# Attention periods of one long kernel: output sums taken from a rotation of three exponent banks, turned 256 columns at a time, and the row of maxima sent one period later

## The chip, the cores and the metric

One NeuronCore of a Trainium2 chip runs one program, of 34,356 recorded instructions. The metric is device time in microseconds, the median of repeated executions. Before the change it is 1423.86 us (three runs, 1423.84 to 1426.14).

## What is computed

Four layers follow each other, A, B, A, B, each added to its input. A is sliding-window attention over 2048 tokens with 576 features, 32 heads of 18, a window of 256; B multiplies the two-dimensional real Fourier transform by a given filter and transforms back. The weights of both A layers are the same, as are the filters of both B layers.

```python
def _A_ref(x, wqkv, wo):
    B, S, D = x.shape
    H = 32; Dh = D // H; W = 256
    qkv = (lambda x, *d: x.transpose(*d))((x @ wqkv).reshape(B, S, 3, H, Dh), 2, 0, 3, 1, 4)
    q, k, v = qkv[0], qkv[1], qkv[2]
    scores = jnp.einsum("bhqd,bhkd->bhqk", q, k) * (Dh ** -0.5)
    idx = jnp.arange(S)
    mask = (idx[:, None] - idx[None, :] >= 0) & (idx[:, None] - idx[None, :] < W)
    scores = jnp.where(mask[None, None], scores, -1e9)
    p = _softmax(scores, axis=-1)
    o = jnp.einsum("bhqk,bhkd->bhqd", p, v)
    return (lambda x, *d: x.transpose(*d))(o, 0, 2, 1, 3).reshape(B, S, D) @ wo
...
x = x + _A_ref(_layernorm(x, axis=-1), A_wqkv, A_wo)
x = x + _B_ref(_layernorm(x, axis=-1), B_w_r, B_w_i)
x = x + _A_ref(_layernorm(x, axis=-1), A_wqkv, A_wo)
x = x + _B_ref(_layernorm(x, axis=-1), B_w_r, B_w_i)
```

The change touches only the attention of the two A layers.

## The kernel before

**Tiles.** An A layer treats its 32 heads as 8 groups n of 4, and the 2048 tokens as 16 tiles of 128; x = 16 n + i counts both, 128 in all. For each x there are four heads (two `pair` by two `hp`), and for each head two products. `score_max` (L1176 on) multiplies queries by keys into a PSUM bank S, up to 128x384, and VectorE (DVE) takes each row's masked maximum out of it: a scan, which also writes its 128x384 by-product to a scratch tile `jk` that nobody reads, and a reading of the engine's accumulator into `m`. The maxima of four tiles are transposed on TensorE (PE) by `m_rows` (L1196), negated on ScalarE (ACT), and sent by DMA into row 63 of the queries, so that the second product already has the maximum subtracted. `exps` (L1206) makes that second product, keys by queries, in a PSUM bank E; ACT exponentiates it into SBUF (P), and GpSimd (POOL) cuts it to the window. `part` (L1228) multiplies P by the values, extended by a column of ones, and accumulates in one bank U: 19 rows for each head, 128 columns for each tile, so U holds four tiles. When these are complete (one x in four) DVE transposes all 512 columns to `us`. `divide` takes the reciprocal of the sums of exponents (DVE) and multiplies (POOL), `back` transposes again (DVE), `store` sends the result.

**Periods.** `mixed()` interleaves this by hand; the order in which the code issues instructions is the order on each engine. A period p handles two x. In it stand 8 scores for x + 10 (LEAD = 10, so maxima are ten tiles ahead of the exponents), 8 exponents, and up to 14 half steps of the query and key projection of later groups (`pj` and `pk`, matmuls with 64 of the 128 rows each). At its end come the 32 matmuls into U (`pv`, for the two x before). There are 59 periods (MIX = 118) in each layer A; p = 0 has no U matmuls, p = 2 to 48 carry projection steps and end with U matmuls, and p = 49 to 58 have no steps left. A period's end is called even or odd by p. At even ends before the change, U is complete and transposed, and `m_rows` runs; `divide` follows in the middle of the next period, `back` at that period's (odd) end, `store` in the middle of the one after. Lists named early, mid and end hold such later work by period. Ahead of `mixed`, `opening` makes the first ten tiles' maxima among projection steps; its fourth score of each tile uses U's bank. Behind `mixed`, a short loop does the last ten tiles.

**PSUM.** Eight banks are shared: S three, pj one, E two, U one, pk one. A matmul into a bank waits until that bank has been read by the instruction that empties it: for S the scan of three scores ago, for E the exponent of two ago. U stays one bank through the whole stage, zeroed once per layer by ACT (`sums`), since only 19 of each 32 rows are written and the transpose reads all.

Of the kernel before, what the change touches and what calls it, by code (L numbers as in the profile page):

```python
# [18 lines left out]
NT = 16  # L19
# [846 lines left out]
def layer_a(tc, ident, eps, bp, big, src, dst, wqk_d, wv_d, wo_d, dc_d, gc_d, dram, copy, wvs, second, spectral, share):  # L866
# [17 lines left out]
    if True:  # L884
# [191 lines left out]
        with ExitStack() as c2:  # L1076
# [19 lines left out]
            def proj(i, c, bank=0):  # L1096
# [5 lines left out]
                def mm(s, k, half=None):  # L1102
# [5 lines left out]
                    if s == 0 and half is None:  # L1108
                        box["ps"] = pp.tile([128, 512], F32, tag="E" if bank else "pj", name=f"pj{i}_{c}", bufs=2 if bank else 1)
                    elif s == 0:  # L1110
                        box[half] = pp.tile([128, 512], F32, tag=("pj", "pk")[half], name=f"{('pj', 'pk')[half]}{i}_{c}", bufs=1)
# [63 lines left out]
            def score_max(x, pair, hp):  # L1175

                n, i = divmod(x, NT)
                c, t = divmod(i, 4)
                q, k = qs[n % 2], ks_[n % 2]
                if (n, c) not in ms:  # L1180
                    ms[n, c] = wp.tile([128, 2, 2, 4], F32, tag="m", name=f"m{n}_{c}", bufs=3)
                lo, hi = max(0, i - 2) * 128, (i + 1) * 128
                N = hi - lo
                b = 64 * hp
                four = x < LEAD and pair == hp == 1
                ps = pp.tile([128, 512], F32, tag="U" if four else "S", name=f"S{x}_{pair}_{hp}", bufs=1 if four else 3)
                T.matmul(ps[:, 0:N], q[b:b + 63, pair, i * 128:i * 128 + 128], k[b:b + 63, pair, lo:hi], start=True, stop=True)  # L1187
                jk = wp.tile([128, 384], BF, tag="jk", name=f"jk{x}_{pair}_{hp}", bufs=2)
                V.tensor_tensor_reduce(out=jk[:, 0:N], in0=ps[:, 0:N], in1=mask[:, 384 - N:384], scale=1.0, scalar=-3e38,  # L1189
                                       op0=ALU.add, op1=ALU.max, accum_out=ms[n, c][:, pair, hp, t:t + 1])  # L1190

            def turned(name):

                return pp.tile([128, 4, 128], F32, tag="E", name=name, bufs=2)
# [12 lines left out]
            def exps(x, pair, hp):  # L1207
# [9 lines left out]
                ps = pp.tile([128, 512], F32, name=f"E{x}_{hl_}", **(dict(tag="S", bufs=3) if pair and NX - LEAD <= x else dict(tag="E", bufs=2)))  # L1217
# [9 lines left out]

            def part(x, half):  # L1228
                n, i = divmod(x, NT)

                e = i - i % 2
                j = (i - 1, i - 2 + 2 * (i % 2))[half]
                q0 = e if j < i else i
                q1 = e + 2 if i - 1 == j else q0 + 1
                for h in range(4):
                    if j >= 0:
                        T.matmul(U[32 * h:32 * h + 19, (q0 % 4) * 128:(q0 % 4) * 128 + 128 * (q1 - q0)], vts[n][:, j, h],  # L1237
                                 pt[n, j][:, h, (q0 - j) * 128:(q1 - j) * 128],
                                 start=j == max(e - 1, 0), stop=j == i or (i == e and j == i - 2), skip_group_check=True)
                if half and i % 4 == 3:  # L1240
                    us[n, i // 4] = u = wp.tile([128, NT, 32], F32, tag="us", name=f"us{n}_{i}", bufs=1)
                    V.transpose(u, U.rearrange("r (p n) -> r n p", n=NT))  # L1242

            def pv(x):
                part(x, 0)
                part(x, 1)
# [3 lines left out]
            def divide(n, c):  # L1250
                u = us[n, c]
                rc = wp.tile([128, NT, 1], F32, tag="rc", name=f"rc{n}_{c}", bufs=2)
                V.reciprocal(rc, u[:, :, 18:19])
                (V if n == NQ - 1 else P).tensor_mul(u[:, :, 0:18], u[:, :, 0:18], rc.to_broadcast([128, NT, 18]))

            def back(n, c):
                os[n, c] = o = wp.tile([128, NT, 32], F32, tag="o", name=f"o{n}_{c}", bufs=2)
                V.transpose(o, us[n, c])
# [68 lines left out]
            us, U = {}, None  # L1327

            def sums():
                nonlocal U  # L1330
                U = pp.tile([128, 512], F32, tag="U", name="U", bufs=1)
                A.activation(U, eps.to_broadcast([128, 512]), AF.Copy, scale=0.0)

            def mixed():
# [11 lines left out]
                for p in range(last):  # L1346
# [9 lines left out]
                    run(early, p)  # L1356
                    for i, (f, *a) in enumerate(some):
# [8 lines left out]
                        if i == 0 and p == 0:  # L1366
                            remainders()
                        if i % 2 == 0 and step:
                            pj[at + n](0)
# [12 lines left out]
                    if p == 0:  # L1382
                        sums()
# [3 lines left out]
                    if p % 2 == 0:  # L1387
                        m_rows(*divmod((2 * p + LEAD + 1) // 4, 4))
                        if p:
                            n, c = divmod((2 * p - 1) // 4, 4)  # L1390
                            plan(mid, p + 1, divide, n, c)
# [6 lines left out]
                    behind(2 * p + 1)  # L1398
                assert at == len(pj)
# [43 lines left out]
            for t in range(MIX, NX + 2):  # L1443
                loads(t)
                for pair in range(2):
# [5 lines left out]
                    if pair == 0 and t - 2 < NX:  # L1451
                        pv(t - 2)
# [8 lines left out]
            def bank(tag, name):  # L1461
                return pp.tile([128, 512], F32, tag=tag, name=name, bufs=dict(pj=1, E=2, S=3)[tag])
# [62 lines left out]
```

## Time and profile before

The profiled execution took 1426.9 us by its own clock, of which 1425.2 us are the span that the trace covers. Its mean granted TensorE clock is 0.963 of full speed.

| | of the span |
|---|---|
| layer A's first mixed stage, p = 2 to 48 | 138.8 to 410.8 us |
| its ten periods without projection steps | 410.8 to 478.5 us |
| the second layer's mixed stage | 867.9 to 1140.6 us, then to 1208.9 us |
| chain that ended last, by engine | PE 73%, ACT 14%, DMA 6%, DVE 3% |
| chain, by line | U L1237 13%, E L1219 11%, P (the exponent) L1220 10%, S L1187 5% |
| the scan, L1189 | 1,024 of them, 497.4 us busy, mean 524 ns |
| the exponent, L1220 | 1,024 of them, 442.2 us busy, mean 471 ns |

In the rows of the trace each instruction stands with its start in us from the beginning of the span, its time, engine, line, operation, and result and operands by name (out<-in); the bracket at a row's end gives the wait before it and what ended it. In the waits, "PE E L1219 <- ACT P L1220: 23.3, 91, 0.5" reads: PE's instructions for E at line 1219 were idle 23.3 us in all, 91 times, because ACT's P at line 1220 was not done, at most 0.5 us at a time. PEld are the weight loads, which run beside matmuls. DVE_READ_ACCUMULATOR2 is the reading behind a scan.

### The profile page before, as it was taken

How to read it: one execution, taken by the hardware profiler on the slowest of the kernel's cores; microseconds unless marked ns; L12 is line 12 of the kernel's file. 1: busy time of each engine (PE TensorE's matmuls, PEld its weight loads, DVE VectorE, ACT ScalarE, POOL GpSimd, SP SyncE). 2: the span in 40 equal slices, each digit the busy share in tenths (PEclk: the TensorE clock that was granted, in tenths of full speed). 3: DMA queues.
4: the chain of work that ended last, by engine and by line, in shares of the span. 5: the costliest groups of instructions: out<-in, count | busy, mean ns of one | idle time of the engine just before them, and what ended most of it. 6: DMA issues, size and time to landing. Idle time of an engine off the chain costs nothing.

```text
span 1425.2 us, 34356 instructions
## 1 busy us (share of the span) xinstructions
PE 1342.7 (94%) x11555; PEld 984.8 (69%) x11555; DVE 956.4 (67%) x3132; ACT 813.2 (57%) x1946; POOL 772.5 (54%) x1248
## 2 busy tenths in 40 slices
PE   9999999999999999999999999999999998999998
PEld 8985555555554589975899865555555544698587
DVE  5428777877776577766663167787788766566855
ACT  5624777777765635443355217777777755575223
POOL 2266677777654534467221385677767655312721
PEclk9999999999987799999999999999999976999999
DMA  6757565755555537678863475656554646488875
GB/s 198 213 179 213 168 199 173 219 178 158 173 169 165 170 95 245 196 251 257 273 229 76 141 205 166 189 178 181 173 174 159 183 142 201 135 272 307 296 226 173
DMA packets 179493, 274.31 MB, mean 192 GB/s; under 512 B 67743, under 2 KB 77727, under 8 KB 177989
## 3 DMA queue, kind: packets, MB, share of 16 engines
q1 hardware_dynamic: 167007, 243.63, 54.6%
q0 software_dynamic: 4656, 13.44, 3.6%
q10 hardware_dynamic: 7654, 15.03, 3.0%
q8 instruction: 93, 1.52, 0.5%
q14 instruction: 83, 0.68, 0.2%
HBM read 164.54 MB, written 114.81 MB: 196 GB/s over the span
## 4 chain that ended last, share of the span: by engine, by line
PE 73%; ACT 14%; DMA 6%; DVE 3%; issue 2%; SPq 1%; POOL 0%; ACTq 0%; DVEq 0%
PE U L1237 13%; PE E L1219 11%; ACT P L1220 10%; PE vps L1005 8%; PE pj L1115 8%; PE ops L802 6%; PE S L1187 5%; PE pk L1115 4%; PE po L274 4%; PE pq L524 3%; PE p L503 2%; PE pf L274 2%; PE pi L600 2%; ACT sg L1136 2%; PE pz L312 1%
## 5 line engine op out<-in xcount | busy, mean ns | idle before, releaser
L1189 DVE CUSTOM_DVE_ANT_0 jk<-S,mask 128x384 bf16<-128x384 f32 (+2 forms) x1024 | 497.4, 524 | 105.7 <-PE S L1187 56.3
L1220 ACT ACTIVATE P<-E 128x384 f32<-128x384 f32 (+2 forms) x1024 | 442.2, 471 | 135.7 <-PE E L1219 69.1
L1219 PE MATMUL E<-qs,ks 64*128 64x384 f32 (+2 forms) x1024 | 385.4, 403 | 54.2 <-ACT P L1220 50.5
L1187 PE MATMUL S<-ks,qs 63*128 63x384 f32 (+2 forms) x1024 | 321.1, 373 | 0.8 <-DVE m L1189 0.6
L1219 PEld LDWEIGHTS E<-qs,ks 64*128 64x128 f32 x1024 | 188.9, 191 | 181.1 <-ACT P L1220 156.2
L1222 POOL TENSOR_SCALAR_AFFINE_SELECT P<-P 128x512 f32<-128x512 f32 x256 | 162.4, 634 | 242.8 <-ACT P L1220 230.8
L1237 PE MATMUL U<-P,vq 128*19 128x128 f32 (+1 forms) x3840 | 208.2, 360 | 0.4 <-POOL P L1222 0.2
L1187 PEld LDWEIGHTS S<-ks,qs 63*128 63x128 f32 x1024 | 175.9, 191 | 41.9 <-DVE m L1189 17.8
L1237 PEld LDWEIGHTS U<-P,vq 128*19 128x19 f32 x3840 | 105.5, 106 | 101.6 <-issue 51.1
L1115 PE MATMUL pj<-xh,wqh 64*128 64x512 f32 (+1 forms) x360 | 152.9, 425 | 0.0
L1225 POOL TENSOR_SCALAR_AFFINE_SELECT P<-P 128x512 f32<-128x512 f32 x224 | 143.7, 642 | 0.0
L1115 PE MATMUL pj<-xh,wql 64*128 64x512 f32 (+1 forms) x360 | 142.2, 433 | 0.0
L1115 PE MATMUL pj<-xl,wqh 64*128 64x512 f32 (+1 forms) x288 | 125.6, 436 | 0.0
L802 PE MATMUL ops<-oroom 128*128 128x290 f32 (+1 forms) x812 | 113.9, 297 | 2.9 <-DVE ofree L825 1.7
L802 PEld LDWEIGHTS ops<-oroom 128*128 128x128 f32 x812 | 110.4, 189 | 3.5 <-ACT ofree L836 2.5
L1242 DVE STREAM_TRANSPOSE us<-U 128x512 f32<-128x512 f32 x64 | 45.9, 717 | 73.2 <-PE U L1237 73.1
L1115 PE MATMUL pk<-xh,wqh 64*128 64x512 f32 x230 | 92.0, 400 | 0.0
L1115 PE MATMUL pk<-xh,wql 64*128 64x512 f32 x230 | 90.2, 396 | 0.0
L1189 DVE DVE_READ_ACCUMULATOR2_ANT m<- 128x1 f32 x1024 | 84.9, 83 | 0.0
L1115 PE MATMUL pk<-xl,wqh 64*128 64x512 f32 x184 | 73.2, 398 | 0.0
L1115 PEld LDWEIGHTS pj<-xh,wqh 64*128 64x128 f32 (+1 forms) x360 | 67.0, 186 | 7.1 <-issue 1.3
L1115 PEld LDWEIGHTS pj<-xh,wql 64*128 64x128 f32 (+1 forms) x360 | 66.9, 186 | 5.5
(519 smaller groups left out, 2599.2 us busy)
## 6 DMA issues: line engine op xcount, KB each, us to landing
qk_d<-sg SPq DMA_DIRECT2D x56, 512.0 KB
qs<-qk_d SPq DMA_DIRECT2D x384, 72.0 KB
ks<-qk_d SPq DMA_DIRECT2D x348, 72.0 KB
op_d<-o SPq DMA_DIRECT2D x56, 256.0 KB
v_d<-vt SPq DMA_DIRECT2D x32, 304.0 KB
vq<-v_d SPq DMA_DIRECT2D x16, 608.0 KB
wt<-in_w SPq DMA_DIRECT2D x16, 580.0 KB
ofree<-x SPq DMA_DIRECT2D x16, 580.0 KB
```

The source lines that it names most:

```text
L274: T.matmul(ps[:, c, 0:NF], tail[r] if si == 4 else hl_(si), dcs[b // 2][r, b % 2], start=mi == si == 0, stop=si == 4)
L802: self.nc.tensor.matmul(self.ps[u][n][:, 0:self.n], x, self.w[p][:, (2 * wk + n) * self.n:(2 * wk + n + 1) * self.n], start=first and i == ...
L1005: T.matmul(ps[:, n, 0:288], xT(xk, c), w[:, wk, n * 288:(n + 1) * 288], start=i == 0, stop=i == len(ks) - 1)
L1115: T.matmul(ps.rearrange("r (n p) -> r n p", n=NT) if second else ps, w[r, wk], x[r], start=s == 0, stop=s == len(ks) - 1)
L1187: T.matmul(ps[:, 0:N], q[b:b + 63, pair, i * 128:i * 128 + 128], k[b:b + 63, pair, lo:hi], start=True, stop=True)
L1189: V.tensor_tensor_reduce(out=jk[:, 0:N], in0=ps[:, 0:N], in1=mask[:, 384 - N:384], scale=1.0, scalar=-3e38, op0=ALU.add, op1=ALU.max, accu ...
L1219: T.matmul(ps[:, 0:nq], k[b:b + 64, pair, j * 128:j * 128 + 128], q[b:b + 64, pair, j * 128:j * 128 + nq], start=True, stop=True)
L1220: A.activation(p[:, hl_, 0:nq], ps[:, 0:nq], AF.Exp, scale=SC)
L1222: P.affine_select(out=p[:, :, 0:128], in_=p[:, :, 0:128], pattern=[[0, 4], [1, 128]], compare_op=ALU.is_ge, fill=0.0, base=0, channel_mult ...
L1225: P.affine_select(out=p[:, :, 256:384], in_=p[:, :, 256:384], pattern=[[0, 4], [-1, 128]], compare_op=ALU.is_gt, fill=0.0, base=0, channel ...
L1237: T.matmul(U[32 * h:32 * h + 19, (q0 % 4) * 128:(q0 % 4) * 128 + 128 * (q1 - q0)], vts[n][:, j, h], pt[n, j][:, h, (q0 - j) * 128:(q1 - j) ...
L1242: V.transpose(u, U.rearrange("r (p n) -> r n p", n=NT))
```

## The change

- **Banks.** pj, pk one each and S three stay. U has no bank of its own any more; E has three instead of two. Each period takes a fresh U out of the rotation of E (out of pk's bank behind `mixed`). The fourth score in `opening` uses pk's bank.
- **U by period.** U holds two tiles, 256 columns, and is transposed at the end of every period but p = 0: 128 columns of `us` rows at a time. Its matmuls load 32 weight columns instead of 19 (the following 13 of the next head beside the 19 wanted), so all 128 rows are written and nothing is zeroed. `us` gets two buffers, and its layout has each half in runs of 16, which `back` undoes with a pattern of four dimensions.
- **Division.** The reciprocal is written in place, and `divide` moves from the middle of the next period to a place behind its first score, as does the list "early" with `pack`.
- **Maxima.** `m_rows` moves from the even end to the odd end after it, and takes its bank out of S (out of E while fewer than 70 projection steps are done).
- **Scratch.** `jk` has one buffer instead of two.

```diff
@@ -1106,7 +1106,7 @@
                     if opens and s == 7 and c == 2 and 0 < i < 8:
                         w_split(i + 1)
                     if s == 0 and half is None:
-                        box["ps"] = pp.tile([128, 512], F32, tag="E" if bank else "pj", name=f"pj{i}_{c}", bufs=2 if bank else 1)
+                        box["ps"] = pp.tile([128, 512], F32, tag="E" if bank else "pj", name=f"pj{i}_{c}", bufs=3 if bank else 1)
                     elif s == 0:
                         box[half] = pp.tile([128, 512], F32, tag=("pj", "pk")[half], name=f"{('pj', 'pk')[half]}{i}_{c}", bufs=1)
                     w = wt[i][0] if p == "h" else wt[i][1]
@@ -1183,15 +1183,15 @@
                 N = hi - lo
                 b = 64 * hp
                 four = x < LEAD and pair == hp == 1
-                ps = pp.tile([128, 512], F32, tag="U" if four else "S", name=f"S{x}_{pair}_{hp}", bufs=1 if four else 3)
+                ps = pp.tile([128, 512], F32, tag="pk" if four else "S", name=f"S{x}_{pair}_{hp}", bufs=1 if four else 3)
                 T.matmul(ps[:, 0:N], q[b:b + 63, pair, i * 128:i * 128 + 128], k[b:b + 63, pair, lo:hi], start=True, stop=True)
-                jk = wp.tile([128, 384], BF, tag="jk", name=f"jk{x}_{pair}_{hp}", bufs=2)
+                jk = wp.tile([128, 384], BF, tag="jk", name=f"jk{x}_{pair}_{hp}", bufs=1)
                 V.tensor_tensor_reduce(out=jk[:, 0:N], in0=ps[:, 0:N], in1=mask[:, 384 - N:384], scale=1.0, scalar=-3e38,
                                        op0=ALU.add, op1=ALU.max, accum_out=ms[n, c][:, pair, hp, t:t + 1])
 
             def turned(name):
 
-                return pp.tile([128, 4, 128], F32, tag="E", name=name, bufs=2)
+                return pp.tile([128, 4, 128], F32, tag="E" if done < 70 else "S", name=name, bufs=3)
 
             def m_rows(n, c):
                 q = qs[n % 2]
@@ -1214,7 +1214,7 @@
                     pt[n, j] = wp.tile([128, 4, 384], F32, tag="P", name=f"P{n}_{j}", bufs=6)
                 p = pt[n, j]
 
-                ps = pp.tile([128, 512], F32, name=f"E{x}_{hl_}", **(dict(tag="S", bufs=3) if pair and NX - LEAD <= x else dict(tag="E", bufs=2)))
+                ps = pp.tile([128, 512], F32, name=f"E{x}_{hl_}", **(dict(tag="S", bufs=3) if pair and NX - LEAD <= x else dict(tag="E", bufs=3)))
                 b = 64 * hp
                 T.matmul(ps[:, 0:nq], k[b:b + 64, pair, j * 128:j * 128 + 128], q[b:b + 64, pair, j * 128:j * 128 + nq], start=True, stop=True)
                 A.activation(p[:, hl_, 0:nq], ps[:, 0:nq], AF.Exp, scale=SC)
@@ -1225,6 +1225,8 @@
                         P.affine_select(out=p[:, :, 256:384], in_=p[:, :, 256:384], pattern=[[0, 4], [-1, 128]], compare_op=ALU.is_gt,
                                         fill=0.0, base=0, channel_multiplier=1)
 
+            us, U = {}, None
+
             def part(x, half):
                 n, i = divmod(x, NT)
 
@@ -1234,12 +1236,18 @@
                 q1 = e + 2 if i - 1 == j else q0 + 1
                 for h in range(4):
                     if j >= 0:
-                        T.matmul(U[32 * h:32 * h + 19, (q0 % 4) * 128:(q0 % 4) * 128 + 128 * (q1 - q0)], vts[n][:, j, h],
-                                 pt[n, j][:, h, (q0 - j) * 128:(q1 - j) * 128],
+                        v = vts[n].rearrange("p b h e -> p (b h e)")[:, 19 * (4 * j + h):min(19 * (4 * j + h) + 32, 76 * NT)]
+                        T.matmul(U[32 * h:32 * h + v.shape[1], (q0 - e) * 128:(q1 - e) * 128], v, pt[n, j][:, h, (q0 - j) * 128:(q1 - j) * 128],
                                  start=j == max(e - 1, 0), stop=j == i or (i == e and j == i - 2), skip_group_check=True)
-                if half and i % 4 == 3:
-                    us[n, i // 4] = u = wp.tile([128, NT, 32], F32, tag="us", name=f"us{n}_{i}", bufs=1)
-                    V.transpose(u, U.rearrange("r (p n) -> r n p", n=NT))
+                if half and i % 2:
+                    c, k = i // 4, i // 2 % 2
+                    if k == 0:
+                        us[n, c] = wp.tile([128, NT, 32], F32, tag="us", name=f"us{n}_{c}", bufs=2)
+                    V.transpose(us[n, c][:, 8 * k:8 * k + 8].rearrange("r b (a p) -> r (b a) p", a=2), U[:, 0:256].rearrange("r (p n) -> r n p", n=NT))
+
+            def sums(tag, x):
+                nonlocal U
+                U = pp.tile([128, 512], F32, tag=tag, name=f"U{x}", bufs=3 if tag == "E" else 1)
 
             def pv(x):
                 part(x, 0)
@@ -1249,13 +1257,13 @@
 
             def divide(n, c):
                 u = us[n, c]
-                rc = wp.tile([128, NT, 1], F32, tag="rc", name=f"rc{n}_{c}", bufs=2)
-                V.reciprocal(rc, u[:, :, 18:19])
+                rc = u[:, :, 18:19]
+                V.reciprocal(rc, rc)
                 (V if n == NQ - 1 else P).tensor_mul(u[:, :, 0:18], u[:, :, 0:18], rc.to_broadcast([128, NT, 18]))
 
             def back(n, c):
                 os[n, c] = o = wp.tile([128, NT, 32], F32, tag="o", name=f"o{n}_{c}", bufs=2)
-                V.transpose(o, us[n, c])
+                V.transpose(o.rearrange("r n (k p) -> r k n p", k=2), us[n, c].rearrange("r (k b) (a p) -> r k (b a) p", k=2, a=2))
 
             def store(n, c, engines=None):
                 o = os[n, c].rearrange("r n p -> r (n p)")
@@ -1324,13 +1332,6 @@
                 for lag, f in zip((1, 3, 4), (divide, back, store)):
                     steps.setdefault(k + lag, []).append((f, n, c))
 
-            us, U = {}, None
-
-            def sums():
-                nonlocal U
-                U = pp.tile([128, 512], F32, tag="U", name="U", bufs=1)
-                A.activation(U, eps.to_broadcast([128, 512]), AF.Copy, scale=0.0)
-
             def mixed():
                 nonlocal done
                 last = MIX // 2
@@ -1353,7 +1354,6 @@
                         some += [(score_max, y, 0, 1), (exps, x, 0, 0), (score_max, y, 1, 1), (exps, x, 1, 0),
                                  (exps, x, 0, 1), (score_max, y, 0, 0), (exps, x, 1, 1), (score_max, y, 1, 0)]
                     n = 0
-                    run(early, p)
                     for i, (f, *a) in enumerate(some):
                         if i in (0, 8):
                             loads(2 * p + i // 8)
@@ -1363,8 +1363,9 @@
                             pj[at + n](1)
                             n += 1
                         f(*a)
-                        if i == 0 and p == 0:
+                        if i == 0:
                             remainders()
+                            run(early, p)
                         if i % 2 == 0 and step:
                             pj[at + n](0)
                         if i == 7:
@@ -1379,16 +1380,17 @@
                             plan(mid, p + 1, f)
                         plan(mid, p + 2, send)
                     ended.clear()
-                    if p == 0:
-                        sums()
+                    if p:
+                        sums("E", p)
                     for x in (2 * p - 2, 2 * p - 1):
                         if x > 0 and x % NT:
                             pv(x)
-                    if p % 2 == 0:
-                        m_rows(*divmod((2 * p + LEAD + 1) // 4, 4))
+                    if p % 2:
+                        m_rows(*divmod((2 * p + LEAD - 1) // 4, 4))
+                    else:
                         if p:
                             n, c = divmod((2 * p - 1) // 4, 4)
-                            plan(mid, p + 1, divide, n, c)
+                            plan(early, p + 1, divide, n, c)
                             plan(end, p + 1, back, n, c)
                             plan(mid, p + 2, store, n, c)
                             if c == 3:
@@ -1396,6 +1398,7 @@
                                     plan(early, p + 4 + h, pack, n, h)
                     run(end, p)
                     behind(2 * p + 1)
+                m_rows(*divmod((2 * last + LEAD - 1) // 4, 4))
                 assert at == len(pj)
                 for d, lags in ((mid, (1, 4)), (end, (3,)), (early, (2, 3))):
                     for k, p in enumerate(sorted(d)):
@@ -1449,6 +1452,8 @@
                     for f, *a in steps.pop(now, ()):
                         f(*a)
                     if pair == 0 and t - 2 < NX:
+                        if t % 2 == 0:
+                            sums("pk", t)
                         pv(t - 2)
                         if t % 4 == 1 and t - 2 < NX - 4:
                             later(now, *divmod(t // 4 - 1, 4))
@@ -1459,7 +1464,7 @@
                 behind(t)
             assert not due and not steps
             def bank(tag, name):
-                return pp.tile([128, 512], F32, tag=tag, name=name, bufs=dict(pj=1, E=2, S=3)[tag])
+                return pp.tile([128, 512], F32, tag=tag, name=name, bufs=1 if tag == "pj" else 3)
 
             out.early(0, [bank(k, f"ops0_{k}") for k in ("pj", "S")], slice(0, 4))
             divide(NQ - 1, 3)
```

In the diff `sums` is defined further up than before (its old definition, from the hunk at L1324, goes), and two hunks at its end take U out of pk behind `mixed` and give the next layer's banks their new counts.

The orders below show the same places of the first layer before and after. A row has the line, the operation, the result's and operands' names (with running numbers) and the shape; x4 means four like it. First PE at the end of the even period p = 4, from the last score to the middle of the next period. Before:

```order
L1187 MATMUL S_1_0_2077<-ks_1061,qs_1059 128x384
L1237 MATMUL U<-P_5_1822,vq_1436 19x256 x4
L1237 MATMUL U<-P_4_1776,vq_1436 19x128 x4
L1237 MATMUL U<-P_6_1887,vq_1436 19x256 x4
L1237 MATMUL U<-P_7_1939,vq_1436 19x128 x4
L1199 MATMUL tpm_0_2099<-ident,m_0_1882 16x128
L1187 MATMUL S_0_1_2109<-ks_1061,qs_1059 128x384
L1219 MATMUL E_0_2114<-qs_1058,ks_1060 128x384
L1187 MATMUL S_1_1_2117<-ks_1061,qs_1059 128x384
```

And after:

```order
L1187 MATMUL S_1_0_2080<-ks_1061,qs_1059 128x384
L1240 MATMUL U_2084<-P_5_1823,vq_1436 32x256 x4
L1240 MATMUL U_2084<-P_4_1777,vq_1436 32x128 x4
L1240 MATMUL U_2084<-P_6_1884,vq_1436 32x256 x4
L1240 MATMUL U_2084<-P_7_1933,vq_1436 32x128 x4
L1187 MATMUL S_0_1_2106<-ks_1061,qs_1059 128x384
L1219 MATMUL E_0_2113<-qs_1058,ks_1060 128x384
L1187 MATMUL S_1_1_2116<-ks_1061,qs_1059 128x384
```

The transpose of the maxima (tpm) is gone from this end; it stands behind the U matmuls of the odd end now, one period later.

Second, DVE at the same even end, from the last scan on; a row of L1189 with jk is a scan, the one with m alone the reading. Before:

```order
L1189 ISA jk_1_0_2079,m_0_1882<-S_1_0_2077,mask 128x384
L1189 ISA m_0_1882 128x1
L1242 STREAM_TRANSPOSE us_7_2097<-U 128x512
L1189 ISA jk_0_1_2111,m_1_2108<-S_0_1_2109,mask 128x384
L1189 ISA m_1_2108 128x1
L1189 ISA jk_1_1_2119,m_1_2108<-S_1_1_2117,mask 128x384
L1189 ISA m_1_2108 128x1
```

And after:

```order
L1189 ISA jk_1_0_2082,m_0_1877<-S_1_0_2080,mask 128x384
L1189 ISA m_0_1877 128x1
L1246 STREAM_TRANSPOSE us_1_1987<-U_2084 128x256
L1189 ISA jk_0_1_2108,m_1_2105<-S_0_1_2106,mask 128x384
L1189 ISA m_1_2105 128x1
L1261 RECIPROCAL us_1_1987<-us_1_1987 128x16
L1189 ISA jk_1_1_2118,m_1_2105<-S_1_1_2116,mask 128x384
L1189 ISA m_1_2105 128x1
```

The transpose is half as wide, and the reciprocal has come forward to a place behind the first scan (it stood behind the fourth).

Third, DVE at the odd end after that, p = 5. Before:

```order
L1189 ISA jk_1_0_2193,m_1_2108<-S_1_0_2191,mask 128x384
L1189 ISA m_1_2108 128x1
L1258 STREAM_TRANSPOSE o_1_2212<-us_7_2097 128x512
L1189 ISA jk_0_1_2222,m_1_2108<-S_0_1_2220,mask 128x384
L1189 ISA m_1_2108 128x1
```

And after:

```order
L1189 ISA jk_1_0_2189,m_1_2105<-S_1_0_2187,mask 128x384
L1189 ISA m_1_2105 128x1
L1246 STREAM_TRANSPOSE us_2_2209<-U_2192 128x256
L1266 STREAM_TRANSPOSE o_1_2217<-us_1_1987 128x2x16x16
L1189 ISA jk_0_1_2227,m_1_2105<-S_0_1_2225,mask 128x384
L1189 ISA m_1_2105 128x1
```

A half transpose of U stands ahead of `back` (L1266), and both ahead of the next scan.

Two waits change with the banks. On PE, exponent 2 of a period (the name E_2) waited for ACT's reading of the bank two exponents back; now U is among the three, and E_2 waits for DVE, that is for the transpose. And on DVE each scan carries a wait for DVE's own count: in before the count that it names lies one or two completions ahead of the instruction just before it, and after the change it is the reading just before it in 841 of 1,024 scans, and an earlier one in the others.

## The prediction, made before the changed kernel was run

> **What bounds the kernel now.** I read the busy times first, then the waits, then the mixed stage by stretches, and last single rows of it.
>
> ```profile
> span 1425.2 us, 34356 instructions
> PE 1342.7 (94%) x11555; PEld 984.8 (69%) x11555; DVE 956.4 (67%) x3132; ACT 813.2 (57%) x1946; POOL 772.5 (54%) x1248
> ```
>
> PE looks like the bound, but the edits lie in the two mixed stages (one for each layer A), so these are read by themselves. The rows give start and end, length, then busy time and instructions of PE, PEld, DVE, ACT and POOL, the granted clock, DMA share and GB/s.
>
> ```profile
> 138.80:410.80 272.00, 252.18 (x2801) 157.83 (x2799) 215.32 (x822) 202.70 (x471) 198.05 (x276) 1.00 0.58 182
> 410.80:478.50 67.70, 61.32 (x459) 32.12 (x460) 46.88 (x177) 38.87 (x93) 35.31 (x52) 0.71 0.55 169
> 867.90:1140.60 272.70, 252.88 (x2805) 157.91 (x2807) 215.54 (x823) 203.30 (x471) 193.81 (x268) 1.00 0.57 173
> 1140.60:1208.90 68.30, 61.70 (x455) 31.77 (x454) 47.16 (x177) 39.07 (x93) 35.31 (x52) 0.71 0.54 166
> ```
>
> The first and third stretch are the 47 periods (p = 2 to 48, from one group of U matmuls to the next) that still carry projection steps: 272.0 / 47 = 5.79 us each, with PE idle for 20 us in all. The second and fourth are the ten periods without them, 6.8 us each at a clock of 0.71. DVE is busy 79% of the first stretch, 4.6 us of each period. PE's idle time, in the first layer from 140 to 465 us:
>
> ```profile
> PE E L1219 <- ACT P L1220: 23.3, 91, 0.5
> ```
>
> So PE waits for one thing, an exponent bank that ACT has yet to read: with two banks the matmul of exponent 7 of a period waits until exponent 5 is read. **But DVE has little to spare**, and how closely it packs its maxima is the point on which I rest the forecast:
>
> ```profile
> 253.14 0.08 DVE L1189 DVE_READ_ACCUMULATOR2_ANT m<- 128x1 f32 x1
> 253.14 0.55 DVE L1189 CUSTOM_DVE_ANT_0 jk<-S,mask 128x384 bf16<-128x384 f32 x1
> 253.62 0.08 DVE L1189 DVE_READ_ACCUMULATOR2_ANT m<- 128x1 f32 x1
> 253.62 0.25 DVE L1253 RECIPROCAL rc<-us 128x16 f32<-128x16 f32 x1
> 253.78 0.49 DVE L1189 CUSTOM_DVE_ANT_0 jk<-S,mask 128x384 bf16<-128x384 f32 x1
> ```
>
> A maximum is two instructions, the scan (0.55) and the reading of its accumulator (0.08). The next instruction starts together with the reading, so scans follow each other every 0.48 us; the reciprocal adds 0.16.
>
> **The change, part by part. jk with one buffer.** A scan may now write jk only when the one before has finished. The built program shows it: each scan has a wait on DVE's own semaphore, in an instruction of its own in front; before, that wait names a point one or two completions ahead of the predecessor and is always past; in the change 841 of 1,024 scans wait for the reading right before them, 13 of 16 in two full periods. No scan of before does this. The nearest rows are the same pair of instructions at another place, followed by one that waits for the reading in the same way (its line has one such wait instruction in the trace):
>
> ```profile
> 1306.45 0.46 DVE L838 CUSTOM_DVE_ANT_0 ofree<-ofree 128x288 f32<-128x288 f32 x1
> 1306.83 0.09 DVE L838 DVE_READ_ACCUMULATOR2_ANT ofree<- 128x1 f32 x1
> 1307.02 0.16 DVE L848 TENSOR_TENSOR ofree<-ofree 128x1 f32<-128x1 f32 x1
> ```
>
> After the reading's end (1306.92) 0.10 us pass. So the pitch becomes 0.48 + 0.08 + 0.10 = 0.67 us (of unrounded times). The ends: nothing (0.48), if the wait is met early; 0.60, if only the 0.03 us pass that lie between a reciprocal and the multiplication that waits for it without an instruction in between (482.30 to 482.34):
>
> ```profile
> 482.05 0.25 DVE L1253 RECIPROCAL rc<-us 128x16 f32<-128x16 f32 x1
> 482.34 0.46 DVE L1254 TENSOR_TENSOR us<-us,rc 128x288 f32<-128x288 f32 x1
> ```
>
> I take 0.67, the row with the same kind of wait. The Trainium skill says the opposite (VectorE: DVE Perf Modes, "The DRAIN you can't avoid"): the engine empties after every operation anyway, and a semaphore costs nothing extra. By that the sum would be the first rival's; the trace does not bear it out, since a scan starts 0.08 us ahead of the end of the reading.
>
> **The transposes.** 64 of 512 columns become 128 of 256.
>
> ```profile
> L1242 DVE STREAM_TRANSPOSE us<-U 128x512 f32<-128x512 f32 x64 | 45.9, 717 | 73.2 <-PE U L1237 73.1
> L1258 DVE STREAM_TRANSPOSE o<-us 128x512 f32<-128x512 f32 x64 | 45.3, 708 | 9.0 <-POOL us L1254 8.5
> L1189 DVE CUSTOM_DVE_ANT_0 jk<-S,mask 128x384 bf16<-128x384 f32 x896 | 456.2, 550 | 82.3 <-PE S L1187 54.3 <-PE E L1219 17.9 <-PE pk L1115 4.0
> L1189 DVE CUSTOM_DVE_ANT_0 jk<-S,mask 128x256 bf16<-128x256 f32 x64 | 24.6, 409 | 9.7 <-PE pk L1115 7.6 <-PE E L1219 1.3 <-PE S L1187 0.7
> ```
>
> Both scans together give 141 ns for 128 columns (1.1 ns each), so half a transpose is 717 - 270, about 0.45 us. The pattern of runs of 16 in back is not in the trace; U is read with a stride in the first row and costs 9 ns more than the plain one, so I take 0.71 for back, at most twice that.
>
> **What a period becomes.** The order shows two kinds. In each, PE's eighth score must wait until the fifth scan has given its bank back; then come the last score, the U matmuls, and the next transpose. The rows for these links:
>
> ```profile
> 250.33 0.38 PE L1237 MATMUL U<-P,vq 128*19 128x128 f32 x5
> 250.78 0.72 DVE L1242 STREAM_TRANSPOSE us<-U 128x512 f32<-128x512 f32 x1 [0.79 <-PE U L1237]
> 251.42 0.52 DVE L1189 CUSTOM_DVE_ANT_0 jk<-S,mask 128x384 bf16<-128x384 f32 x1
> 253.28 0.18 PEld L1187 LDWEIGHTS S<-ks,qs 63*128 63x128 f32 x1 [0.17 <-DVE m L1189]
> 254.99 0.33 PE L1187 MATMUL S<-ks,qs 63*128 63x384 f32 x1
> 255.25 1.50 PE L1237 MATMUL U<-P,vq 128*19 128x256 f32 x32
> 256.51 0.71 DVE L1258 STREAM_TRANSPOSE o<-us 128x512 f32<-128x512 f32 x1 [0.48 <-POOL us L1254]
> 257.16 0.56 DVE L1189 CUSTOM_DVE_ANT_0 jk<-S,mask 128x384 bf16<-128x384 f32 x1
> ```
>
> The next scan starts 0.64 after a whole transpose has started, so 0.64 - 0.27 = 0.37 after a half one, and 0.65 after back. A score's load starts 0.06 after the reading (253.22 to 253.28); the U matmuls start 0.26 after the last score, 0.37 where that score had to wait and is filled anew (0.44 instead of 0.33, as behind a wait at 253.28); they take 1.50; the transpose follows 0.07 later.
>
> - After an even period's end (half transpose, scan, reciprocal, then scans 0.67 apart): the fifth scan starts at 0.37 + 0.48 + 0.16 + 3 x 0.67 = 3.02, and the next transpose at 3.02 + 0.56 + 0.06 + 0.37 + 1.50 + 0.07 = **5.58 us**.
> - After an odd one (half transpose, back, then scans): back stood under the U matmuls and now waits in DVE's queue behind the transpose, and eight scans wait behind both. The fifth starts at 0.37 + 0.65 + 4 x 0.67 = 3.70, and the period is **6.26 us**.
>
> Of 47 periods 24 are of the second kind, 23 of the first; in 6 of these the scans are those of a new group of heads (128 and 256 columns), where DVE does not bind and I put 5.4 us, below the 5.79 mean. 24 x 6.26 + 17 x 5.58 + 6 x 5.4 = 277.5 us against 272.0: **+5.5 us a layer, +11 in all**. Ends: with 0.60, A is 5.37 and B 5.98, and with 5.3 for the six the sum is 266.6, -11 in all; without the wait, the first rival.
>
> In the ten periods without steps the U matmuls run at half clock in eight:
>
> ```profile
> 430.09 2.68 PE L1237 MATMUL U<-P,vq 128*19 128x256 f32 x32
> ```
>
> 1.2 us more: 5.58 + 6.26 + 4 x (6.78 + 7.46) = 68.8 us, less 0.5 for a group's start, against 67.7 and 68.3: **+1 in both**.
>
> **The third exponent bank** takes one exponent's wait (0.48) off the end of a period, but a period that DVE sets doesn't become shorter by it. U holds one of the three until its transpose; exponent 2 is behind it, at 0.52 us after the U matmuls, ahead of where PE stands (its E at 257.73 in the period above, 1.0 after). No cost while DVE starts the transpose in time.
>
> **The rest.** The zeroing of U goes, for which PE waited:
>
> ```profile
> PE tpm L1199 <- ACT U L1332: 1.6, 2, 0.8
> ```
>
> -1.6 us, and -0.5 for two halved transposes at the layers' ends. A weight load of 32 columns for 19 is hidden under the U matmuls. The row of maxima goes out a period later, with one period (5.6 us at least) of slack in place of two; the longest landing on the chain is 6.5:
>
> ```profile
> 125.48 6.52 DMA qs<-mt
> ```
>
> I take none; were all 60 that late, 0.9 each is 54 us, a far end that I leave out. POOL's multiplication comes earlier, and nobody waits for it. The opening's scans (2.7 us for four at 0.67) stay under PE's seven steps.
>
> **Sum**: 11 + 1 - 1.6 - 0.5 = +10 us, on the profiled execution's own 1426.9 us about 1437; that one lies 3.0 above the median of 1423.86, so the forecast is **1434 us**.
>
> **Rivals.** *The wait costs nothing* (by the skill's sentence above, and as the change's title means it): DVE keeps 0.48, and each period that PE ended waiting gains up to an exponent, 0.4 us of 0.48 in 94 periods and in 20: -46 - 2, or **1376 us**. For it speaks the 23.3 us row; against it the start of a scan ahead of the reading's end. *The wait costs only 0.03* (pitch 0.60): -11, -4 for 20 periods of 0.2, -2: **1407 us**. *The clock falls earlier*: it is 1.00 to 410 us and 0.71 where steps are missing; periods that are longer by DVE leave PE less busy, and if ten more periods a layer lose 1.2 us each, +24: **1458 us**; the same holds if back's runs double its time (0.7 in 48 periods and ten, +40 at most). It decides from the point where the steps get fewer (p over 42). *The change does not do what it says*: U in the rotation takes back the third bank, and PE waits at exponent 2 for the transpose; that gives the forecast's time too, with E waiting for DVE.
>
> **How the numbers follow.** The forecast's case (1421 to 1450) has 0.54, no cost 0.13, 0.03 us 0.14, clock or runs 0.19. Faster by over 0.2% (about what a measurement can tell from no change): 0.13 + 0.14 and 0.08 of the forecast's spread, 0.35; within, 0.08; slower 0.57. The range, 1396 to 1458, leaves out the first rival and what lies above the last.
>
> **What would show it.** Right: scans 0.66 to 0.67 us apart, DVE over 90% busy or held by its own readings in the mixed stage, periods that alternate near 5.6 and 6.3, and PE waiting for maxima (S for DVE) where it waited for exponents. Wrong: scans still 0.48 apart, or periods of one length near 5.4. The transpose at 0.45, back at 0.71 and the clock to 410 us are each to be read off alone.

## The result, and the profile after

The changed kernel takes 1462.2 us (median of 4 runs, 1457.43 to 1464.3) against 1423.85 beside it: a ratio of 1.0268, 95% interval 1.0233 to 1.0302. It is slower, as forecast, but by 38 us where 10 were forecast, and 4 us above the range's end of 1458. The profiled execution took 1462.71 us, with a span of 1461.0.

The page's first lines and its chain, after:

```profile
span 1461.0 us, 34480 instructions
...
PE 1382.8 (95%) x11555; PEld 1015.9 (70%) x11555; DVE 1007.0 (69%) x3196; ACT 790.2 (54%) x1944; POOL 774.8 (53%) x1248
...
PE 66%; DVE 20%; issue 5%; ACT 5%; DMA 3%; SPq 1%; POOL 0%; DVEq 0%; ACTq 0%; POOLq 0%
```

DVE has gone from 3% of the chain to 20%. The busy share hides it, 69% for 67%. The stretches that answer to those shown before (columns as there), and DVE's scans within one of them:

```profile
142.80:424.60 281.80, 268.36 (x2801) 168.72 (x2800) 232.63 (x846) 194.28 (x472) 199.00 (x276) 1.00 0.55 174
424.60:493.00 68.40, 61.66 (x458) 32.16 (x458) 51.77 (x183) 37.50 (x93) 35.75 (x53) 0.72 0.52 161
888.90:1171.10 282.20, 269.25 (x2805) 169.76 (x2804) 232.70 (x846) 194.40 (x472) 194.81 (x268) 1.00 0.54 168
1171.10:1240.60 69.50, 61.92 (x458) 32.25 (x458) 51.73 (x183) 37.72 (x93) 35.79 (x53) 0.72 0.52 159
```

```profile
163.29 0.08 DVE L1189 DVE_READ_ACCUMULATOR2_ANT m<- 128x1 f32 x1
163.52 0.56 DVE L1189 CUSTOM_DVE_ANT_0 jk<-S,mask 128x384 bf16<-128x384 f32 x1
164.00 0.08 DVE L1189 DVE_READ_ACCUMULATOR2_ANT m<- 128x1 f32 x1
164.23 0.56 DVE L1189 CUSTOM_DVE_ANT_0 jk<-S,mask 128x384 bf16<-128x384 f32 x1
164.71 0.08 DVE L1189 DVE_READ_ACCUMULATOR2_ANT m<- 128x1 f32 x1
```

A scan itself takes what it took, 0.56 us, but the next starts 0.71 us after it where it was 0.48: 0.15 us lie between the end of a reading (164.08) and the next scan. The periods alternate; the U matmuls of two in a row start at

```profile
160.13 1.51 PE L1240 MATMUL U<-P,vq 128*32 128x256 f32 x32
...
165.93 1.51 PE L1240 MATMUL U<-P,vq 128*32 128x256 f32 x32
...
172.32 1.51 PE L1240 MATMUL U<-P,vq 128*32 128x256 f32 x32
```

which is 5.79 us after an even end and 6.39 after an odd one. Is DVE then full? For the stretch from 148.5 to 424.6 us (276.1 us) the page by stretches gives 227.94 us of DVE busy, and the groups of DVE's instructions by line (busy, mean ns, then the idle time ahead) are:

```profile
L1189 DVE CUSTOM_DVE_ANT_0 jk<-S,mask 128x384 bf16<-128x384 f32 (+2 forms) x369 | 194.5, 527 | 44.4 <-DVE m L1189 1.0 <-PE pk L1115 0.9 <-PE E L1219 0.5
L1189 DVE DVE_READ_ACCUMULATOR2_ANT m<- 128x1 f32 x368 | 30.5, 83 | 0.0
L1246 DVE STREAM_TRANSPOSE us<-U 128x256 f32<-128x256 f32 x46 | 20.5, 445 | 3.8 <-PE U L1240 3.8
L1266 DVE STREAM_TRANSPOSE o<-us 128x512 f32<-128x512 f32 x23 | 15.4, 669 | 0.0
```

227.9 busy, 44.4 ahead of scans and 3.8 ahead of transposes make 276.1: all of it. Of the 44.4 only 2.4 are put down to a named instruction; the other 42 us are the pauses between a reading and the next scan. DVE is busy 83% of this stretch and does not look full, but apart from the 3.8 us ahead of transposes it has no time left.

### The profile page after: what moved, and what is told of

The parts are those of the page before. It is cut to its first block, busy times and chain, and to the rows that moved or that the text cites. A ratio compares the mean times of both kernels' runs of the same rounds, so it can differ in the third digit from the quotient of the medians.

```text
span 1461.0 us, 34480 instructions
## 1 busy us (share of the span) xinstructions
PE 1382.8 (95%) x11555; PEld 1015.9 (70%) x11555; DVE 1007.0 (69%) x3196; ACT 790.2 (54%) x1944; POOL 774.8 (53%) x1248
## 4 chain that ended last, share of the span: by engine, by line
PE 66%; DVE 20%; issue 5%; ACT 5%; DMA 3%; SPq 1%; POOL 0%; DVEq 0%; ACTq 0%; POOLq 0%
DVE jk L1189 15%; PE S L1187 10%; PE vps L1005 8%; PE pj L1115 8%; PE U L1240 7%; PE ops L802 6%; PE pk L1115 5%; PE E L1219 4%; PE po L274 4%; ACT P L1220 3%; PE pq L524 2%; PE p L503 2%; PE pf L274 2%; PE pi L600 2%; DVE o L1266 1%
## 5 line engine op out<-in xcount | busy, mean ns | idle before, releaser
L1189 DVE CUSTOM_DVE_ANT_0 jk<-S,mask 128x384 bf16<-128x384 f32 (+2 forms) x1024 | 541.4, 529 | 125.6 <-PE S L1187 2.8
L1220 ACT ACTIVATE P<-E 128x384 f32<-128x384 f32 (+2 forms) x1024 | 416.8, 478 | 184.3 <-PE E L1219 106.7
L1187 PE MATMUL S<-ks,qs 63*128 63x384 f32 (+2 forms) x1024 | 387.2, 411 | 40.6 <-DVE m L1189 30.7
L1219 PE MATMUL E<-qs,ks 64*128 64x384 f32 (+2 forms) x1024 | 330.4, 380 | 5.4 <-ACT P L1220 4.1
L1187 PEld LDWEIGHTS S<-ks,qs 63*128 63x128 f32 x1024 | 182.9, 192 | 202.2 <-DVE m L1189 176.6
L1219 PEld LDWEIGHTS E<-qs,ks 64*128 64x128 f32 x1024 | 185.1, 193 | 47.6 <-ACT P L1220 24.2
L1240 PE MATMUL U<-P,vq 128*32 128x256 f32 (+2 forms) x3840 | 206.3, 357 | 11.0 <-DVE us L1246 10.1
L1240 PEld LDWEIGHTS U<-P,vq 128*32 128x32 f32 (+1 forms) x3840 | 115.5, 117 | 90.9 <-issue 46.1
L1115 PE MATMUL pj<-xl,wqh 64*128 64x512 f32 (+1 forms) x288 | 121.8, 423 | 0.0
L1189 DVE DVE_READ_ACCUMULATOR2_ANT m<- 128x1 f32 x1024 | 85.0, 83 | 0.0
L1246 DVE STREAM_TRANSPOSE us<-U 128x256 f32<-128x256 f32 x128 | 57.1, 446 | 39.2 <-PE U L1240 38.9
```

Of the source, the lines that this page charges most:

```text
L1115: T.matmul(ps.rearrange("r (n p) -> r n p", n=NT) if second else ps, w[r, wk], x[r], start=s == 0, stop=s == len(ks) - 1)
L1219: T.matmul(ps[:, 0:nq], k[b:b + 64, pair, j * 128:j * 128 + 128], q[b:b + 64, pair, j * 128:j * 128 + nq], start=True, stop=True)
L1220: A.activation(p[:, hl_, 0:nq], ps[:, 0:nq], AF.Exp, scale=SC)
L1240: T.matmul(U[32 * h:32 * h + v.shape[1], (q0 - e) * 128:(q1 - e) * 128], v, pt[n, j][:, h, (q0 - j) * 128:(q1 - j) * 128], start=j == max( ...
L1246: V.transpose(us[n, c][:, 8 * k:8 * k + 8].rearrange("r b (a p) -> r (b a) p", a=2), U[:, 0:256].rearrange("r (p n) -> r n p", n=NT))
```

## The experiments

Each kernel was timed beside the kernel before; ratios are to that one, and medians of different rows of runs can differ by some microseconds.

**e1: two scratch buffers.** They are of bytes instead of bf16, so that two take the room of one:

```diff
-                jk = wp.tile([128, 384], BF, tag="jk", name=f"jk{x}_{pair}_{hp}", bufs=1)
+                jk = wp.tile([128, 384], mybir.dt.uint8, tag="jk", name=f"jk{x}_{pair}_{hp}", bufs=2)
```

> The changed kernel with two scratch buffers (bytes instead of bf16, so that two take the room of one). Theory 1, the single scratch buffer spaces the scans: their pitch goes from 0.71 back to 0.48 us, the two openings lose 2 to 5 us together, the mixed periods fall from 6.00 us on average to about 5.45, and the time is about 1405 us (1385 to 1425). Rival A, the order at the odd ends or U in the exponents' rotation sets the period: the pitch is 0.48, the openings are back, but the odd-end periods stay above 6 us and the time above 1440. Rival B, the scans are slow for another reason (the wait instructions themselves): pitch 0.6 or more, time as after, 1460.

Measured: **1346.87 us**, ratio 0.9477 (0.9453 to 0.9502), 115 us below the change as it is. A few rows of DVE:

```profile
160.67 0.56 DVE L1189 CUSTOM_DVE_ANT_0 jk<-S,mask 128x384 uint8<-128x384 f32 x1
161.14 0.08 DVE L1189 DVE_READ_ACCUMULATOR2_ANT m<- 128x1 f32 x1
161.14 0.55 DVE L1189 CUSTOM_DVE_ANT_0 jk<-S,mask 128x384 uint8<-128x384 f32 x1
161.62 0.08 DVE L1189 DVE_READ_ACCUMULATOR2_ANT m<- 128x1 f32 x1
161.62 0.55 DVE L1189 CUSTOM_DVE_ANT_0 jk<-S,mask 128x384 uint8<-128x384 f32 x1
```

The pitch (from one scan's start to the next one's) is 0.48 again. Theory 1 is right in kind, and even its expectation (1385 to 1425) was too timid. The stretches of e1 show where the time went:

```profile
135.90:389.40 253.50, 245.84 (x2806) 163.90 (x2805) 209.71 (x846) 191.26 (x472) 198.04 (x277) 0.99 0.63 200
389.40:444.50 55.10, 51.91 (x453) 27.57 (x453) 45.49 (x180) 37.27 (x94) 35.38 (x53) 0.91 0.64 200
829.20:1076.70 247.50, 243.73 (x2802) 162.19 (x2801) 209.85 (x846) 190.88 (x472) 193.67 (x268) 1.00 0.63 196
1076.70:1130.50 53.80, 50.69 (x454) 27.48 (x453) 45.39 (x181) 37.20 (x94) 35.41 (x53) 0.94 0.65 204
```

Against before, the periods with projection steps gain 18.5 and 25.2 us, and the ten without them 12.6 and 14.5; there the granted clock is 0.91 and 0.94 where it was 0.71. How much of these 27 us is the clock's and how much the shorter waits' was not separated. The openings (first score to p = 1) are 3.6 and 6.1 us shorter than before, and the ends behind the mixed stage 2.8 and 3.0 longer. In the periods with steps PE is now busy for 245.84 of 253.50 and 243.73 of 247.50 us.

**e2: the kernel before with one scratch buffer.** The same line with `bufs=1` for `bufs=2`, nothing else.

> The kernel before with one scratch buffer, nothing else. Theory 1: pitch 0.71, openings 2 to 5 us longer together, and in the mixed stage DVE sets the periods, 6.2 us after an even end (whole transpose ahead of the scans) and 5.55 after an odd one, 5.87 on average against 5.79: about 1437 us (1430 to 1450). Rival B (the single buffer costs nothing): 1424.

Measured: **1484.16 us**, ratio 1.0448 (1.0421 to 1.0474). The buffer alone costs 64 us even without the rest, where I expected 13: the mixed stretches take 291.9 and 292.1 us against 272, and the openings are some 9 and 5 us longer. The single buffer costs time by itself, without the rest of the change.

**e9 and e10: is it the buffer, or the byte type?** e9 has no scratch at all, each scan writing over the scores in its own bank; e10 has one buffer of bytes.

```diff
# e9
-                jk = wp.tile([128, 384], BF, tag="jk", name=f"jk{x}_{pair}_{hp}", bufs=1)
-                V.tensor_tensor_reduce(out=jk[:, 0:N], in0=ps[:, 0:N], in1=mask[:, 384 - N:384], scale=1.0, scalar=-3e38,
+                V.tensor_tensor_reduce(out=ps[:, 0:N], in0=ps[:, 0:N], in1=mask[:, 384 - N:384], scale=1.0, scalar=-3e38,
# e10
-                jk = wp.tile([128, 384], BF, tag="jk", name=f"jk{x}_{pair}_{hp}", bufs=1)
+                jk = wp.tile([128, 384], mybir.dt.uint8, tag="jk", name=f"jk{x}_{pair}_{hp}", bufs=1)
```

> The changed kernel without a scratch tile: each scan writes its by-product over the scores in its own PSUM bank (float32), so no scan waits for the one before, and no byte type is used. Theory 1: scans 0.48 us apart and 1340 to 1355 us, as e1. If writing to PSUM is dearer, the scans themselves grow longer than 0.55 us and the time lies above that. Rival (e1's gain comes from the byte type): 1460.

> The changed kernel with one scratch buffer as it has, but of bytes. Theory 1: 1462 within 5 us, scans 0.71 us apart: the type does nothing, the second buffer everything. Rival (the byte type makes the scans faster): below 1420.

Measured: e9 **1360.72 us** (0.9569, 0.9534 to 0.9604), e10 **1460.9** (1.0261, 1.0226 to 1.0296). One buffer of bytes is as slow as one of bf16, so the type does nothing. Without a scratch the wait is gone. A scan that writes float32 to PSUM takes longer, and e9 stays 0.9%, some 13 us, behind e1. Two scans of e9, and the reading between them:

```profile
160.66 0.59 DVE L1188 CUSTOM_DVE_ANT_0 S<-S,mask 128x384 f32<-128x384 f32 x1
161.17 0.14 DVE L1188 DVE_READ_ACCUMULATOR2_ANT m<- 128x1 f32 x1
161.17 0.59 DVE L1188 CUSTOM_DVE_ANT_0 S<-S,mask 128x384 f32<-128x384 f32 x1
```

The scans lie 0.51 us apart, 0.03 more than in e1, and the reading grows from 0.08 to 0.14. That the longer scans cost the 13 us is not shown: the two mixed stretches of e9 take 250.1 and 250.2 us, in sum no more than e1's, and of the 7.5 us by which the profiled spans differ, 6.6 lie in the second layer's ten periods without steps (60.4 us at a clock of 0.83, against 53.8 at 0.94).

**e5: what gains the 73 us of e1?** e1, but U has a bank of its own and the exponents two (three more lines set the same numbers of banks):

```diff
-                U = pp.tile([128, 512], F32, tag=tag, name=f"U{x}", bufs=3 if tag == "E" else 1)
+                U = pp.tile([128, 512], F32, tag="U", name=f"U{x}", bufs=1)
...
-                ps = pp.tile([128, 512], F32, name=f"E{x}_{hl_}", **(dict(tag="S", bufs=3) if pair and NX - LEAD <= x else dict(tag="E", bufs=3)))
+                ps = pp.tile([128, 512], F32, name=f"E{x}_{hl_}", **(dict(tag="S", bufs=3) if pair and NX - LEAD <= x else dict(tag="E", bufs=2)))
```

> As e1_jk_two (changed kernel, two scratch buffers, 1347 us), but U keeps a bank of its own and the exponents have two again; half transposes, back, maxima and division stay as changed. If the rotation of three banks is what the 73 us of e1 come from, the wait of E for ACT returns (0.4 us and more in most periods) and the time is 1395 to 1420. If the halved transposes or the moved division gain them, it stays within 10 us of 1347.

Measured: **1427.56 us**, ratio 1.0038 (1.0019 to 1.0057). All of e1's gain is gone; the halved transposes, the moved division and the later maxima together gain nothing. The periods with projection steps take 272.8 and 273.2 us, against 272.0 and 272.6 before the change. The waits of PE's weight loads from 150 to 382 us (us, times, longest), first of the kernel before, then of e5, then of e1, then of the changed kernel, show the third bank at work:

```profile
PEld E L1219 <- ACT P L1220: 48.4, 106, 0.7
...
PEld S L1187 <- DVE m L1189: 5.3, 29, 0.3
```

```profile
PEld E L1219 <- ACT P L1220: 50.4, 101, 0.7
```

```profile
PEld S L1187 <- DVE m L1189: 18.5, 75, 0.4
PEld E L1219 <- ACT P L1220: 9.3, 37, 0.9
...
PEld E L1219 <- DVE us L1246: 3.4, 20, 0.2
```

```profile
PEld S L1187 <- DVE m L1189: 50.0, 130, 0.5
PEld E L1219 <- ACT P L1220: 5.0, 21, 0.6
PEld E L1219 <- DVE us L1246: 5.0, 20, 0.6
```

So the change does what it says: the wait for ACT falls from 50 us to 9 with three banks, and U in the rotation costs 3. In the changed kernel the weight loads again wait 50 us, now for DVE's maxima ahead of the scores, where the kernel before waited 5.3.

**e3: U's bank behind the mixed stage.**

```diff
-                            sums("pk", t)
+                            sums("E" if t % 4 else "pk", t)
```

> The changed kernel with U of every second pair of tiles behind the mixed stage in a bank of the exponents instead of always pk. If the single pk bank behind a late transpose is what lengthens the two ends (3.9 and 3.8 us), the PE wait of 5.1 us in each goes, and the time falls by 6 to 9 us to about 1454. If the transpose queue of DVE is late anyway for what follows, at most 2 us go.

Measured: 1450.81 us, ratio 1.0198 (1.0173 to 1.0223), 0.7% below the change as it is, or some 10 us. In the changed kernel this row stood at the first layer's end:

```profile
518.11 1.94 PE L1240 MATMUL U<-P,vq 128*32 128x256 f32 x20 [5.08 <-DVE us L1246]
```

The next U needs the single bank of pk, whose transpose stands on DVE behind the splitting of the attention's output (L787 to 789), and the splitting waits for a DMA transfer. In e3 the wait is gone, and the time from the last period's U matmuls to the last group of them falls from 25.1 and 25.0 us to 19.9 and 20.4.

**e4: back ahead of U's transpose at the odd ends**, so that it stands under the U matmuls (`run(end, p)` moved ahead of the matmuls, with one scratch buffer):

```diff
+                    run(end, p)
                     if p:
                         sums("E", p)
...
-                    run(end, p)
                     behind(2 * p + 1)
```

> The changed kernel with the transpose back issued ahead of U's transpose at the odd ends, so that it stands under the U matmuls as before the change. If the queue at the odd ends costs what the order suggests (0.65 us in each of 48 + 10 periods), the periods that begin at an odd end fall from 6.38 to about 5.79 and the time by 28 to 34 us, to about 1430. If the scans behind it take up the slack elsewhere, or back now waits for GpSimd, 10 us or less.

Measured: 1450.75 us, ratio 1.0208 (1.019 to 1.0226): 0.6% or 9 us, not 28 to 34. The period after an odd end stays at 6.38, its U matmuls starting at

```profile
165.95 1.51 PE L1240 MATMUL U<-P,vq 128*32 128x256 f32 x32
...
172.33 1.51 PE L1240 MATMUL U<-P,vq 128*32 128x256 f32 x32
```

That speaks against the prediction's way of reading the odd ends, as a place in a queue: here DVE is full, and gains nothing from another order. DVE's time from 149.0 to 422.7 us is 228.38 busy, 44.9 idle ahead of scans and 0.6 ahead of U's transposes, 273.9 of 273.7 us; what DVE had waited for U (3.8 us in the changed kernel) is all that was to be had, and from the U matmuls of p = 1 to those of p = 48 e4 is 2.4 us shorter in each layer. The other 4 of its 9 us lie outside the mixed stages; the two ends are 0.8 and 0.9 us shorter, and the rest is not explained here.

**e6, e7 and e8: the better version.** e6 is e1 with back moved as in e4, e7 is e6 with e3's bank, e8 is e7 with the maxima at the even ends again:

```diff
-                    if p % 2:
-                        m_rows(*divmod((2 * p + LEAD - 1) // 4, 4))
-                    else:
+                    if p % 2 == 0:
+                        m_rows(*divmod((2 * p + LEAD + 1) // 4, 4))
                         if p:
...
-                m_rows(*divmod((2 * last + LEAD - 1) // 4, 4))
```

> As e1_jk_two, with the transpose back ahead of U's at the odd ends. In e1 periods after an odd end take 5.51 us, after an even one 4.95, and at odd ends the first scan starts 0.98 us after the transpose of U starts instead of 0.37. If with two buffers the order at the odd ends sets the path (scans, eighth score, U), the periods after odd ends fall to about 5.0 and the time by 20 to 28 us, to about 1322. If DVE's total or PE sets them, 8 us or less.

> e6 with the bank of the exponents for every second U behind the mixed stage, as in e3: 8 to 11 us below e6 if the late transpose behind the single bank costs the same there (PE waits 5.1 us in each layer), about 1312; no more than 3 if other work fills it.

> e7 with the maxima sent at the even ends again, one period earlier as before the change. In e1 the exponents wait 1.8 us for the row of maxima in two places, and one landing lay 4 us on the chain: if these go, 2 to 6 us below e7; if the earlier place only moves the waits (tpm behind the scans at a PE that is nearly full), within 2 us of e7.

Measured: 1336.8 (0.9387, 0.9344 to 0.943), 1332.59 (0.9361, 0.9321 to 0.94) and 1330.0 us (0.9359, 0.932 to 0.9398). Back ahead is worth 10 to 13 us (by the medians and by the ratios) and not 20 to 28: the periods after odd ends go from 5.51 to some 5.35 in e6, not to 5.0. The times of the three can't be told apart by these runs, so neither e3's bank nor the earlier maxima is shown to help the whole here. In the profiled executions the ends behind the mixed stage are 4.9 and 4.5 us shorter in e7 than in e6, as in e3. All three beat the kernel before by 6% and the changed one by 9%.

## Why the prediction was right, and where it failed

- **The sign and the mechanism were right.** The single scratch buffer makes each scan wait for the reading ahead of it, DVE becomes the bound, and PE waits for maxima where it waited for exponents. e2 and e10 show that one buffer does it, e1 and e9 that nothing else stands in the way.
- **The pitch was mis-sized: 0.67, measured 0.71.** The row chosen gave 0.10 us from a reading's end to the next instruction; here it is 0.15. The rival of 0.03 us and that of no cost are out. The Trainium skill's sentence that a semaphore between vector operations costs nothing extra (VectorE: DVE Perf Modes, "The DRAIN you can't avoid"), which that page measured on copies, does not hold for a scan behind a reading: 0.71 against 0.48.
- **The mixed stages were mis-sized: +11 forecast, +19.4 measured** (281.87 and 282.18 us from U to U against 271.97 and 272.63). Periods after an even end took 5.79 (forecast 5.58), after an odd one 6.38 (6.26), the six at a new group of heads 5.06 on average (5.4). The term that failed is the pitch: with 0.71 in place of 0.67 the prediction's own links give 5.70 and 6.42, and with 5.06 for the six 281.3 us. That this path (fifth scan, eighth score, U) comes so close is in part luck, because it is not what binds. DVE's own sum is: in a pair of periods 13 scans at 0.71, 3 at 0.48, two halved transposes at 0.37, back at 0.65 and the reciprocal at 0.16 are 12.2 us, and the pair takes 12.18. e4 tells the two readings apart: by the path back's place should matter, and the period stayed at 6.38.
- **The openings: "stay under PE's seven steps" was wrong.** From the first score to p = 1 they grew by 3.5 and 1.1 us. Four scans at 0.71 are 2.8 us, and the tiles there come every 2.4 us before the change (scores at 114.88, 117.23 and 119.62); the seven steps were never set against that. The 1.6 us forecast to be saved on the zeroing of U lie in this stretch too, which grew all the same.
- **The ends behind the mixed stage: -0.5 in all forecast, +3.9 and +3.8 measured.** The last hunks of the diff, U in one bank of pk while DVE's queue waits for a DMA, were not priced. e3 shows it.
- **Right in size:** the ten periods without steps (+1 in both together forecast; +0.7 and +1.2), the halved transpose (0.45; 446 ns, although 141 ns for 128 columns make 282 for 256, and 270 were taken off), back (0.71; 673 ns, so its short runs cost nothing), the clock (1.00 through the 47 periods), and maxima one period later, for whose landing PE never waits in the changed kernel (in e1 it does twice, 1.8 us in all). The total of the ten periods is in part luck: forecast were two at full clock and eight of 6.78 and 7.46, and in the first layer the first five take 5.8 to 6.6 and the last five 7.2 to 7.7.
- **The sum of the terms.** The mixed stages, the openings, the ends and the ten periods make 33.6 of the 35.8 us by which the profiled span grew; the rest lies between and behind the layers. Against the 10 us forecast, the mixed stages are some 8 off, the openings 6, the ends 8 and the ten periods 1: more than half of the miss lies in the openings and the ends, for which the prediction counted no cost at all.
- **The first rival, 1376, was worth more than its price.** It is what happens without the wait, in e1. Its 0.4 us in each of the 94 periods is 38 us, and e1 gains 43.7; in the 20 others it is 8, and e1 gains 27. A granted clock that rises in those was in no rival.

## What to carry to other kernels

A buffer that nobody reads still orders the instructions that write it. Before giving one up for space, look at the waits of the built program, not at what the data needs; here that room was worth 115 us, and a smaller type kept both buffers. And where an engine's instructions follow each other with pauses, add up busy time and pauses: that an engine is 70 or 80% busy doesn't say that it has time left (here 227.9 us busy and 42 us of pauses in 276.1).

## What the runs showed of the hardware

- A scan that must wait for the reading just ahead of it starts 0.15 us after that has ended, and its pitch goes from 0.48 to 0.71, 0.23 us for one dependence: also lost is the 0.08 us by which the next scan otherwise overlaps the reading.
- A scan writing 128x384 float32 back to PSUM takes 0.59 us against 0.55 into SBUF bytes, and its reading 0.14 against 0.08.
- In the ten periods without projection steps the granted clock was 0.71 before, 0.72 after and 0.91 to 0.94 in e1, and they are 27 us shorter in e1 than before. The clock alone does not set their length: at 0.79 they take 69.1 us in e2's first layer and 57.0 in e6's second. What makes the clock fall was not tried.
